# Elementwise work of two fused layers redistributed over VectorE, GpSimd and ScalarE

## The chip, the cores and the metric

One NeuronCore of a Trainium2 chip runs the whole program. The metric is the device time of one execution, in microseconds (us). Its engines are TensorE (matrix products; PE in the profile, PEld for its weight loads), VectorE (DVE), ScalarE (ACT), GpSimd (POOL) and SyncE (SP, which here issues nearly all DMAs). Each engine runs its own instructions strictly in the order of the program and waits on semaphores for the others.

## What is computed

The reference is a causal, windowed attention (4 batches, 8 heads, 576 tokens, head size 64) with a bias by distance, whose output is seen as `x` of 2304 tokens by 512, followed by two layers of the same form:

```
h = x @ w_in            # 512 -> 2048
g = where(h > 0, h, exp(min(h, 0)) - 1)      # layer 0 (ELU)
g = h * (1 / (1 + exp(-h)))                  # layer 1 (SiLU)
x = g @ w_out           # 2048 -> 512
```

The weights come as 64-bit floats. Everything is computed close to fp32 precision.

## The kernel before

**Products in halves.** TensorE multiplies a type that holds fewer bits than fp32. So every operand is split into an upper half (a ScalarE copy into that type) and a lower half (value minus upper half), and each product is three matmuls: upper by upper, upper by lower, lower by upper. For each operand tile there is thus one ScalarE instruction (`gh`, `w1h`, `wah`, ...) and one subtraction (`gl`, `w1l`, `wal`, ...).

**Stages.** The attention runs first and takes about 210 us; the first four feature tiles (`FIRST_F`, of 128 features each) of layer 0 are computed inside it, by `hidden` and `output`. What is left of that for the last token block ends at 240.4 us of the profiled execution. Then come 15 *steps* (the list `steps`, lines 657 and 658). A step is one block `b` of 768 tokens (`BIG`) with a *sweep* of six feature tiles, or four in the last sweep of layer 1. Layer 0 has two sweeps of three steps (steps 0 to 5), layer 1 three sweeps of three steps (steps 6 to 14). A step is a first part with quads and a second part with outputs.

**Quads.** `quad` (line 762) computes two feature tiles of `h` for 768 tokens with seven products in place of eight, as Strassen's scheme in Winograd's form does. The operands are sums of quarters of the weights (`s1` to `s4`, lines 188 to 191, in `part`) and sums of quarters of `x` (`t2`, `t3`, and two in place, lines 689 to 694, in `make`). A step of six features has three quads and 21 products of six matmuls. Each product's result is copied or added up by ScalarE (line 786) or VectorE (line 789).

**Activation.** Each quad gives four half-tiles of 128 features by 384 tokens, a full step twelve. `activate` (line 746) puts for each a chain of four entries in a list, and `chain` (line 740) emits one entry of every open chain after each product: `bent` (exp or sigmoid, line 752), the entry that calls `act` (lines 257 and 258 in layer 0, two VectorE instructions; line 260 in layer 1, one), `upper` (line 755) and `lower` (line 759). `lower` is GpSimd's, except for one half in layer 1.

**Outputs.** `outputs` (line 835 and on) multiplies the six `g` tiles with `w_out` (line 866), in eight groups (layer 0) or six (layer 1) of three pieces each, and adds each group into `acc` (line 879). The order is: `pieces` of the last step that were kept back (`pend`) are mixed among the first products, the last two products of a step among its first pieces.

**Weights.** A list of 64 `tasks` (one per 128-feature tile of `w_in` or `w_out`) goes strictly in order through `load_w` (a 512 KB DMA on SP, four raw buffers, `NRAW`), `rescale` (one GpSimd instruction, line 146, one ScalarE instruction, line 148), `sign` and `join` (VectorE, lines 153 and 158) and `part`. For `w_out` `part` is one upper and one lower half (`w1h`, `w1l`, line 168). For `w_in` two tasks make a *pair*: `wah`, `wal`, then the four sums, then `wb`, `wc`, `wd` with their halves. There is room for three pairs (`PAIRS`) and seven `w_out` tiles (`OUTS`). The room of a pair is given free when the last step of a sweep has used it, that of all `w_out` tiles of a sweep when the last group of that step is begun. So most of the next sweep's weights are made around the boundary between two sweeps: steps 2 and 3, 5 and 6, 8 and 9, 11 and 12. `weight_step` (line 215) is called by `between` after each product or output piece (`calls` counts them) and takes a few stages one task further, seven calls (`LAG`) after the load at the earliest; where a step needs a weight that is not there yet, a loop calls it until it is.

**Sums of x.** `make` (line 673) makes the seven operands of a step from `x`, in two halves `c` of the contraction. `begin` loads a half from DRAM in layer 0 (one buffer, so half 1 is loaded when half 0 is used up) and takes `acc` in layer 1. Its list of entries is emitted three at a time (`POPS`) by `between("y")`. In layer 0 the list begins with 21 empty entries (`POPS * LAG`), and 21 more stand between the two halves. After both, seven `keep` DMAs of 768 KB store the operands for a later step, in layer 0 and where a later step uses them. `make` runs for steps 0, 1, 2 (layer 0) and 6, 7, 8 (layer 1); the other steps reload the kept operands or use those of the step before. Step 0's list is put into the queue before the attention's leftover work is done; those of the others at the start of the outputs of the step before.

Of the kernel before, what the change touches and what calls it, by code (L numbers as in the profile page):

```python
# [13 lines left out]
AF = mybir.ActivationFunctionType  # L14
ALU = mybir.AluOpType
PSUM = bass.MemoryType.PSUM

P = 128
# [4 lines left out]
def f32(ap):  # L23
    return ap.bitcast(F32)
# [18 lines left out]
def attention_elu_silu_kernel(  # L43
# [14 lines left out]
    nc = tc.nc  # L58
# [5 lines left out]
    NKC = DM // P  # L64
# [12 lines left out]
    NRAW = 4  # L77
# [94 lines left out]
    def part(kind, layer, f):  # L172

        if kind == 1 or (layer == 0 and f < FIRST_F):
            top = raws.pop((kind, layer, f))[:, :, 1]
            pool = w_p if layer == 0 and f < FIRST_F else out_p[0]
            weights[kind, layer, f] = halves(pool, f"w{kind}", [(top, NKC * P)], nc.gpsimd)
            return
        if f % 2 == 0:
            t = raws[kind, layer, f]  # L180
            weights[kind, layer, f] = halves(pair_p[0], "wa", [(t[:, :, 1], NKC * P)], nc.gpsimd)
            return

        t0, t1 = raws.pop((kind, layer, f - 1)), raws.pop((kind, layer, f))
        w = NKC * P // 2
        a11, a12, a21, a22 = (f32(t[:, i * w:(i + 1) * w, 1]) for t in (t0, t1) for i in range(2))
        s1, s2, s3, s4 = (f32(t[:, i * w:(i + 1) * w, 0]) for t in (t0, t1) for i in range(2))
        nc.gpsimd.tensor_tensor(s1, a21, a22, op=ALU.add)
        nc.gpsimd.tensor_tensor(s3, a11, a21, op=ALU.subtract)
        nc.gpsimd.tensor_tensor(s2, s1, a11, op=ALU.subtract)  # L190
        nc.gpsimd.tensor_tensor(s4, a12, s2, op=ALU.subtract)
        weights[kind, layer, f] = (
            halves(pair_p[0], "wb", [(t1[:, w:2 * w, 1], w)], nc.vector),
            halves(pair_p[0], "wc", [(t0[:, :, 0], 2 * w)], nc.vector),
            halves(pair_p[0], "wd", [(t1[:, :, 0], 2 * w)], nc.vector))
# [19 lines left out]
    def weight_step(loaded=0, which=(4, 2, 3, 1), lag=1, last=64, apart=(1, 0, 1)):  # L215


        for i in which:
            if (stage[i] < min(last, stage[i - 1]) and (i < len(stages) or fits(stage[i]))
                    and calls[0] >= at[i - 1][stage[i]] + (lag, *apart)[i - 1]):  # L220
                if i == len(stages):
                    made[tasks[stage[i]][0]] += 1
                stages[i - 1](*tasks[stage[i]])
                at[i][stage[i]] = calls[0]
                stage[i] += 1
        while stage[0] < (loaded or min(stage[-1] + NRAW, len(tasks))):
            load_w(*tasks[stage[0]])
            at[0][stage[0]] = calls[0]
            stage[0] += 1
# [417 lines left out]
    def layers(fill):  # L647
# [25 lines left out]
        def make(k):  # L673

            layer, sw, b = steps[k]
            src = {}

            def begin(c):
                if layer == 0:
                    src[c] = t = t_p.tile([P, 2, BIG], F32, tag="xs", name="xs")  # L680
                    nc.sync.dma_start(t, x_dram[b][:, c::2, :])
                else:
                    src[c] = acc[b].rearrange("p (c t) -> p c t", c=NKC)[:, c::2, :]

            def sums(c):
                b11, b12, b21, b22 = (src[c][:, i, j * HALF:(j + 1) * HALF] for i in range(2) for j in range(2))
                t2, t3 = (t_p.tile([P, HALF], F32, tag=t, name=t) for t in ("t2", "t3"))
                src[c] = b11, b21, b22, b21, b12, t2, t3
                nc.gpsimd.tensor_tensor(t3, b22, b12, op=ALU.subtract)
                nc.gpsimd.tensor_tensor(b12, b12, b11, op=ALU.subtract)  # L690
                nc.gpsimd.tensor_tensor(t2, b22, b12, op=ALU.subtract)

            def last_sum(c):
                nc.gpsimd.tensor_tensor(src[c][1], src[c][1], src[c][5], op=ALU.subtract)

            def upper(c, i):
                if c == 0:
                    operand(k, i)
                nc.scalar.activation(combos[k, i][:, 0, c, :], src[c][i], AF.Copy)  # L699

            def lower(c, i):
                t = combos[k, i]
                nc.vector.tensor_tensor(t[:, 1, c, :], src[c][i], f32(t[:, 0, c, :]), op=ALU.subtract)

            def keep(i):
                d = scratch[layer, b, i] = dram_p.tile([P, 4 * HALF], F32, tag=f"d{layer}{b}{i}", name=f"d{layer}{b}{i}")
                nc.sync.dma_start(d, f32(combos[k, i].rearrange("p x c t -> p (x c t)")))

            def spread(c):
                out = [lambda: sums(c)]  # L710
                order = 1, 0, 5, 4, 6, 3, 2
                for x, i in enumerate(order):
                    out.append(lambda i=i: upper(c, i))
                    if x:
                        out.append(lambda i=order[x - 1]: lower(c, i))
                    if x == 2:
                        out.append(lambda: last_sum(c))
                out.append(lambda: lower(c, order[-1]))
# [6 lines left out]
            return begin_first, wait + out  # L725

        def reload(k, i):
            layer, sw, b = steps[k]
# [17 lines left out]
        def activate(layer, src, gh, gl, half, key):  # L746
            tiles = {}
            s = slice(half * HALF, (half + 1) * HALF)

            def bent():  # L750
                tiles["e"] = e = e_p.tile([P, HALF], F32, tag="e", name="e")
                nc.scalar.activation(e, src, AF.Exp if layer == 0 else AF.Sigmoid)  # L752

            def upper():
                nc.scalar.activation(gh[:, s], tiles["e"], AF.Copy)  # L755

            def lower():
                eng = nc.vector if layer == 1 and half == 0 else nc.gpsimd
                eng.tensor_tensor(gl[:, s], tiles["e"], f32(gh[:, s]), op=ALU.subtract)  # L759
            chains.append([bent, lambda: act(layer, src, tiles["e"]), upper, lower])  # L760

        def quad(k, q, last):

# [132 lines left out]

        begin, xs0 = make(0)
        begin()
        xtasks.extend(xs0)
        seq = list(fill)  # L900
        fill.clear()
        for pieces, after, _, _ in seq:
# [101 lines left out]
```

## Time and profile before

| | |
|---|---|
| median of 3 runs | 1026.32 us (1025.3 to 1027.28) |
| the profiled execution, device time | 1027.41 us |
| its span, first to last instruction | 1025.6 us |
| mean granted TensorE clock | 0.937 |
| busy: PE, DVE, ACT, POOL | 900.2, 633.1, 490.6, 427.2 us |
| chain that ended last, shares | PE 51%, DVE 15%, POOL 13%, ACT 9%, issue 7%, DMA 4% |

The busy times are of the whole span. TensorE is the busiest, but its busy time is not all work at full speed: the granted clock (PEclk) tells in tenths or hundredths what share of 2.4 GHz it ran at, and a matmul at 1.2 GHz is counted as busy for twice the time. The chain that ended last names what the end waited for, step by step; a share of VectorE, GpSimd and ScalarE in it means that TensorE stood still for them there.

### The profile page before, as it was taken

Reading aid. Unit: us, or ns where it says so; the run is one execution under the profiler, and the core shown is the slowest. Engines: PE = TensorE matmul, PEld = TensorE weight load, DVE = VectorE, ACT = ScalarE, POOL = GpSimd, SP = SyncE. Lnnn points to the kernel's source line nnn. Section 1 sums busy time; section 2 is a strip of 40 time slices with the busy share of each in tenths; the row PEclk is TensorE's granted clock in tenths of the full one; section 3 lists DMA queues with packets and bytes.
Section 4 is the critical chain, followed back from the end, with each engine's and each line's share of the span. In section 5 each row is a group of like instructions: output and inputs, shape, how many; then the busy total and the mean of one; then the engine's idle time right before and its main releaser. Section 6 shows DMA issues by size and latency. Waiting matters only on the chain.

```text
span 1025.6 us, 15310 instructions
## 1 busy us (share of the span) xinstructions
PE 900.2 (88%) x5520; PEld 798.6 (78%) x5520; DVE 633.1 (62%) x1241; ACT 490.6 (48%) x1155; POOL 427.2 (42%) x514
## 2 busy tenths in 40 slices
PE   6789999874649998897999839899989899999998
PEld 3667767653549998796999839698979698889997
DVE  6876567537666766777354678847377543474443
ACT  6676667534442536353233445555456332444322
POOL 7743333226554345755031763615264301252111
PEclk9889999996789998998999869999989899999999
DMA  9324353031731611236050128051324505024541
GB/s 303 104 73 150 115 156 124 12 113 64 299 118 43 235 31 42 72 116 234 1 216 1 46 93 305 20 215 66 150 82 157 222 3 214 5 78 184 186 184 62
DMA packets 54924, 125.52 MB, mean 122 GB/s; under 512 B 3648, under 2 KB 35648, under 8 KB 54848
## 3 DMA queue, kind: packets, MB, share of 16 engines
q1 hardware_dynamic: 54704, 124.40, 34.0%
q8 instruction: 44, 0.72, 0.3%
q14 instruction: 32, 0.26, 0.1%
q10 hardware_dynamic: 144, 0.13, 0.0%
HBM read 87.56 MB, written 36.96 MB: 121 GB/s over the span
## 4 chain that ended last, share of the span: by engine, by line
PE 51%; DVE 15%; POOL 13%; ACT 9%; issue 7%; DMA 4%; POOLq 0%; DVEq 0%; SPq 0%; ACTq 0%
PE y L866 24%; PE b L779 9%; PE c L779 5%; DVE e L257 3%; PE a L527 3%; DVE e L258 3%; PE h L274 3%; PE y L310 2%; POOL gl L759 2%; PE a L779 2%; DVE wraw L153 2%; DMA wraw<-in_moe_w_out_dram 2%; PE s L449 2%; PE pt L488 2%; ACT e L752 2%
## 5 line engine op out<-in xcount | busy, mean ns | idle before, releaser
L759 POOL TENSOR_TENSOR gl<-e,gh 128x384 fp32r<-128x384 f32 x120 | 131.1, 1095 | 321.6 <-ACT gh L755 297.0
L755 ACT ACTIVATE gh<-e 128x384 fp32r<-128x384 f32 x168 | 86.7, 523 | 103.8 <-DVE e L258 62.7
L866 PE MATMUL y<-w1h,gl 128*128 128x512 f32 (+1 forms) x292 | 115.2, 394 | 2.9 <-DVE gl L759 2.9
L866 PE MATMUL y<-w1h,gh 128*128 128x512 f32 (+1 forms) x292 | 114.8, 393 | 1.4 <-ACT gh L755 1.4
L866 PE MATMUL y<-w1l,gh 128*128 128x512 f32 (+1 forms) x292 | 114.5, 392 | 0.0
L866 PE MATMUL y<-gl,w1h 128*128 128x384 f32 x288 | 100.9, 350 | 15.2 <-POOL gl L759 15.2
L866 PE MATMUL y<-gh,w1h 128*128 128x384 f32 x288 | 100.3, 348 | 9.8 <-ACT gh L755 9.8
L508 POOL TENSOR_SCALAR p<-p,sm 128x192 f32<-128x192 f32 (+1 forms) x144 | 61.5, 445 | 100.7 <-DVE sm L466 90.8
L879 DVE TENSOR_TENSOR acc<-y,acc 128x384 f32<-128x384 f32 (+2 forms) x85 | 50.3, 605 | 81.1 <-PE y L866 81.1
L866 PE MATMUL y<-gh,w1l 128*128 128x384 f32 x288 | 99.8, 347 | 0.0
L257 DVE TENSOR_SCALAR e<-e 128x384 f32<-128x384 f32 (+2 forms) x92 | 51.9, 565 | 52.7 <-ACT e L752 30.9
L462 ACT ACTIVATE p<-p,neg 128x192 f32<-128x192 f32 (+1 forms) x144 | 62.9, 440 | 31.6 <-DVE neg L457 31.6
L153 DVE SCALAR_TENSOR_TENSOR wraw<-wraw 128x512 uint32<-128x512 uint32 x60 | 57.9, 965 | 26.2 <-POOL wraw L146 24.9
L866 PEld LDWEIGHTS y<-gl,w1h 128*128 128x128 f32 x288 | 56.5, 196 | 17.6 <-POOL gl L759 17.5
L786 ACT ACTIVATE hs<-b 128x384 f32<-128x384 f32 x42 | 20.2, 480 | 102.4 <-PE b L779 102.4
L866 PEld LDWEIGHTS y<-w1h,gl 128*128 128x128 f32 x292 | 56.0, 192 | 15.2 <-DVE gl L759 3.8
L752 ACT ACTIVATE e<-hs 128x384 f32<-128x384 f32 x84 | 44.1, 525 | 47.3 <-DVE hs L789 47.0
L866 PEld LDWEIGHTS y<-gh,w1h 128*128 128x128 f32 x288 | 57.0, 198 | 11.1 <-ACT gh L755 11.1
L866 PEld LDWEIGHTS y<-w1h,gh 128*128 128x128 f32 x292 | 56.0, 192 | 11.8 <-ACT gh L755 2.2
L168 POOL TENSOR_TENSOR w1l<-wraw,w1h 128x512 fp32r<-128x512 f32 x28 | 40.1, 1431 | 59.5 <-ACT w1h L167 42.9
L866 PEld LDWEIGHTS y<-w1l,gh 128*128 128x128 f32 x292 | 55.9, 191 | 9.6
L779 PE MATMUL b<-b,wah 128*128 128x384 f32 x168 | 44.0, 340 | 22.1 <-ACT b L699 20.1
(146 smaller groups left out, 2378.4 us busy)
## 6 DMA issues: line engine op xcount, KB each, us to landing
t<-d SPq DMA_DIRECT2D x24, 768.0 KB, 7.3
wraw<-in_moe_w_in_dram SPq DMA_DIRECT2D x32, 512.0 KB, 4.5
d<-t SPq DMA_DIRECT2D x20, 768.0 KB, 8.5
wraw<-in_moe_w_out_dram SPq DMA_DIRECT2D x28, 512.0 KB, 4.1
b<-d SPq DMA_DIRECT2D x18, 768.0 KB, 5.9
d<-b SPq DMA_DIRECT2D x15, 768.0 KB, 4.8
k<-in_k_dram SPq DMA_DIRECT2D x16, 384.0 KB, 5.2
v<-in_v_dram SPq DMA_DIRECT2D x18, 256.0 KB, 2.8
```

Of the source, the lines that this page charges most:

```text
L153: nc.vector.scalar_tensor_tensor(low, top, 0x80000000, low, op0=ALU.bitwise_and, op1=ALU.bitwise_or)
L168: eng.tensor_tensor(lo[:, o:o + w], f32(src), f32(h[:, o:o + w]), op=ALU.subtract)
L257: nc.vector.tensor_scalar(e, e, 1.0, -1.0, op0=ALU.min, op1=ALU.add)
L258: nc.vector.tensor_tensor(e, src, e, op=ALU.max)
L462: nc.scalar.activation(dst, dst, AF.Exp, bias=m, scale=-1.0, accum_out=a)
L508: nc.gpsimd.tensor_scalar(dst, dst, by, 1.0, op0=ALU.mult, op1=ALU.mult)
L752: nc.scalar.activation(e, src, AF.Exp if layer == 0 else AF.Sigmoid)
L755: nc.scalar.activation(gh[:, s], tiles["e"], AF.Copy)
L759: eng.tensor_tensor(gl[:, s], tiles["e"], f32(gh[:, s]), op=ALU.subtract)
L779: nc.tensor.matmul(t[name][:, 0:HALF], a[:, cs], x[:, j, c, :], start=(start and c == 0 and n == 0), stop=(c == 1 and n == 2), skip_group_ ...
L866: nc.tensor.matmul(t["ps"][:, 0:w], l, r, start=(f == 0 and x == 0), stop=(f == n - 1 and x == 2))
L879: nc.vector.tensor_tensor(dst, t["ps"][:, 0:w], dst, op=ALU.add)
```

## The change

All lower halves and sums of the layers that GpSimd made (`w1l`, `wal`, `s1` to `s4`, `gl`, the four sums of `x` per half) become VectorE instructions. GpSimd keeps the scaling of raw weights (line 146), the lower halves of the weights of the first four tiles, and what it did in the attention. In layer 0, two of the four half-tiles of a quad (`below`) get `min(h, 0)` from ScalarE, as minus `relu(-h)`, ahead of the exp, and then one VectorE instruction in place of two. In `weight_step` a raw buffer is loaded again only two calls after its last user was emitted. The list of sums of `x` loses its 21 leading empty entries; step 0's gets six.

```
--- before.py
+++ after.py
@@ -174,21 +174,22 @@
         if kind == 1 or (layer == 0 and f < FIRST_F):
             top = raws.pop((kind, layer, f))[:, :, 1]
             pool = w_p if layer == 0 and f < FIRST_F else out_p[0]
-            weights[kind, layer, f] = halves(pool, f"w{kind}", [(top, NKC * P)], nc.gpsimd)
+            eng = nc.gpsimd if pool is w_p else nc.vector
+            weights[kind, layer, f] = halves(pool, f"w{kind}", [(top, NKC * P)], eng)
             return
         if f % 2 == 0:
             t = raws[kind, layer, f]
-            weights[kind, layer, f] = halves(pair_p[0], "wa", [(t[:, :, 1], NKC * P)], nc.gpsimd)
+            weights[kind, layer, f] = halves(pair_p[0], "wa", [(t[:, :, 1], NKC * P)], nc.vector)
             return
 
         t0, t1 = raws.pop((kind, layer, f - 1)), raws.pop((kind, layer, f))
         w = NKC * P // 2
         a11, a12, a21, a22 = (f32(t[:, i * w:(i + 1) * w, 1]) for t in (t0, t1) for i in range(2))
         s1, s2, s3, s4 = (f32(t[:, i * w:(i + 1) * w, 0]) for t in (t0, t1) for i in range(2))
-        nc.gpsimd.tensor_tensor(s1, a21, a22, op=ALU.add)
-        nc.gpsimd.tensor_tensor(s3, a11, a21, op=ALU.subtract)
-        nc.gpsimd.tensor_tensor(s2, s1, a11, op=ALU.subtract)
-        nc.gpsimd.tensor_tensor(s4, a12, s2, op=ALU.subtract)
+        nc.vector.tensor_tensor(s1, a21, a22, op=ALU.add)
+        nc.vector.tensor_tensor(s3, a11, a21, op=ALU.subtract)
+        nc.vector.tensor_tensor(s2, s1, a11, op=ALU.subtract)
+        nc.vector.tensor_tensor(s4, a12, s2, op=ALU.subtract)
         weights[kind, layer, f] = (
             halves(pair_p[0], "wb", [(t1[:, w:2 * w, 1], w)], nc.vector),
             halves(pair_p[0], "wc", [(t0[:, :, 0], 2 * w)], nc.vector),
@@ -224,6 +225,8 @@
                 at[i][stage[i]] = calls[0]
                 stage[i] += 1
         while stage[0] < (loaded or min(stage[-1] + NRAW, len(tasks))):
+            if not loaded and stage[0] >= NRAW and calls[0] < at[-1].get(stage[0] - NRAW, 0) + 2:
+                break
             load_w(*tasks[stage[0]])
             at[0][stage[0]] = calls[0]
             stage[0] += 1
@@ -686,12 +689,12 @@
                 b11, b12, b21, b22 = (src[c][:, i, j * HALF:(j + 1) * HALF] for i in range(2) for j in range(2))
                 t2, t3 = (t_p.tile([P, HALF], F32, tag=t, name=t) for t in ("t2", "t3"))
                 src[c] = b11, b21, b22, b21, b12, t2, t3
-                nc.gpsimd.tensor_tensor(t3, b22, b12, op=ALU.subtract)
-                nc.gpsimd.tensor_tensor(b12, b12, b11, op=ALU.subtract)
-                nc.gpsimd.tensor_tensor(t2, b22, b12, op=ALU.subtract)
+                nc.vector.tensor_tensor(t3, b22, b12, op=ALU.subtract)
+                nc.vector.tensor_tensor(b12, b12, b11, op=ALU.subtract)
+                nc.vector.tensor_tensor(t2, b22, b12, op=ALU.subtract)
 
             def last_sum(c):
-                nc.gpsimd.tensor_tensor(src[c][1], src[c][1], src[c][5], op=ALU.subtract)
+                nc.vector.tensor_tensor(src[c][1], src[c][1], src[c][5], op=ALU.subtract)
 
             def upper(c, i):
                 if c == 0:
@@ -722,7 +725,7 @@
             out = spread(0) + [lambda: begin(1)] + wait + spread(1)
             if again(k):
                 out += [lambda i=i: keep(i) for i in range(7)]
-            return begin_first, wait + out
+            return begin_first, out
 
         def reload(k, i):
             layer, sw, b = steps[k]
@@ -747,17 +750,29 @@
             tiles = {}
             s = slice(half * HALF, (half + 1) * HALF)
 
+            below = layer == 0 and key[1] % 2 != half
+
             def bent():
                 tiles["e"] = e = e_p.tile([P, HALF], F32, tag="e", name="e")
-                nc.scalar.activation(e, src, AF.Exp if layer == 0 else AF.Sigmoid)
+                if below:
+                    nc.scalar.activation(e, src, AF.Relu, scale=-1.0)
+                    nc.scalar.activation(e, e, AF.Exp, scale=-1.0)
+                else:
+                    nc.scalar.activation(e, src, AF.Exp if layer == 0 else AF.Sigmoid)
+
+            def gated():
+                e = tiles["e"]
+                if below:
+                    nc.vector.scalar_tensor_tensor(e, e, -1.0, src, op0=ALU.add, op1=ALU.max)
+                else:
+                    act(layer, src, e)
 
             def upper():
                 nc.scalar.activation(gh[:, s], tiles["e"], AF.Copy)
 
             def lower():
-                eng = nc.vector if layer == 1 and half == 0 else nc.gpsimd
-                eng.tensor_tensor(gl[:, s], tiles["e"], f32(gh[:, s]), op=ALU.subtract)
-            chains.append([bent, lambda: act(layer, src, tiles["e"]), upper, lower])
+                nc.vector.tensor_tensor(gl[:, s], tiles["e"], f32(gh[:, s]), op=ALU.subtract)
+            chains.append([bent, gated, upper, lower])
 
         def quad(k, q, last):
 
@@ -896,7 +911,7 @@
 
         begin, xs0 = make(0)
         begin()
-        xtasks.extend(xs0)
+        xtasks.extend([None] * (2 * POPS) + xs0)
         seq = list(fill)
         fill.clear()
         for pieces, after, _, _ in seq:
```

## Rows read from the trace of the kernel before

**Rows 1.** section 1 of the page: busy time and span share by engine

```profile
...
PE 900.2 (88%) x5520; PEld 798.6 (78%) x5520; DVE 633.1 (62%) x1241; ACT 490.6 (48%) x1155; POOL 427.2 (42%) x514
...
```

**Rows 2.** stretches: us, busy (instructions) by engine, PEclk, DMA share, GB/s

```profile
...
210.00:240.40 30.40, 24.66 (x96) 19.31 (x95) 14.39 (x17) 10.86 (x21) 14.94 (x16) 0.89 0.28 95
210.00:331.70 121.70, 79.12 (x354) 69.55 (x353) 78.82 (x105) 49.67 (x100) 63.21 (x62) 0.82 0.36 128
...
379.90:500.00 120.10, 104.64 (x542) 100.51 (x542) 81.82 (x122) 50.91 (x101) 61.94 (x60) 0.91 0.28 99
500.00:547.70 47.70, 47.21 (x271) 46.89 (x271) 23.27 (x41) 15.93 (x33) 12.11 (x12) 1.00 0.31 116
547.70:675.20 127.50, 102.30 (x505) 95.06 (x505) 94.37 (x130) 63.98 (x130) 71.35 (x67) 0.88 0.31 112
675.20:721.60 46.40, 46.40 (x236) 42.14 (x235) 27.35 (x41) 25.24 (x53) 16.21 (x14) 1.00 0.33 136
721.60:828.40 106.80, 99.96 (x470) 88.59 (x469) 62.56 (x92) 50.99 (x103) 45.71 (x45) 0.94 0.36 133
...
874.80:925.20 50.40, 48.21 (x235) 43.64 (x234) 32.41 (x47) 22.49 (x46) 21.15 (x21) 0.97 0.12 42
240.40:1025.60 785.20, 692.98 (x3505) 643.22 (x3503) 480.95 (x723) 339.62 (x695) 319.59 (x305) 0.93 0.33 122
...
```

**Rows 3.** line 759: instructions, duration in ns min/median/max, first and last start

```profile
...
L759 POOL TENSOR_TENSOR gl<-e,gh x120: 993/1015/1562, 274.1 to 1011.2; 128x384 fp32r<-128x384 f32 x120
L759 DVE TENSOR_TENSOR gl<-e,gh x48: 542/550/1675, 627.0 to 1009.2; 128x384 fp32r<-128x384 f32 x48
...
```

**Rows 4.** line 168, same columns: lower halves of weights, on both engines

```profile
...
L168 POOL TENSOR_TENSOR w1l<-wraw,w1h x28: 1292/1328/1766, 268.2 to 937.3; 128x512 fp32r<-128x512 f32 x28
L168 POOL TENSOR_TENSOR wal<-wraw,wah x14: 1291/1317/1659, 213.7 to 901.7; 128x512 fp32r<-128x512 f32 x14
L168 DVE TENSOR_TENSOR wbl<-wraw,wbh x14: 440/1058/1300, 221.0 to 907.5; 128x256 fp32r<-128x256 f32 x14
...
L168 DVE TENSOR_TENSOR wdl<-wraw,wdh x14: 677/691/1502, 225.7 to 909.8; 128x512 fp32r<-128x512 f32 x14
...
```

**Rows 5.** groups by line and shape on GpSimd: busy, mean ns, idle before

```profile
...
L188 POOL TENSOR_TENSOR wraw<-wraw 128x256 f32<-128x256 f32 x14 | 15.0, 1073 | 1.5 <-DVE wraw L158 1.5
...
```

**Rows 6.** order of time, 396 to 408: start, us, instruction [idle before <-releaser]

```profile
...
397.76 1.21 POOL L759 TENSOR_TENSOR gl<-e,gh 128x384 fp32r<-128x384 f32 x1
...
398.13 1.26 DVE L258 TENSOR_TENSOR e<-hs,e 128x384 f32<-128x384 f32 x1
...
401.70 0.66 ACT L167 ACTIVATE wch<-wraw 128x512 fp32r<-128x512 f32 x1 [3.29 <-POOL wraw L190]
...
403.10 0.69 DVE L168 TENSOR_TENSOR wdl<-wraw,wdh 128x512 fp32r<-128x512 f32 x1
...
405.30 0.56 DVE L258 TENSOR_TENSOR e<-hs,e 128x384 f32<-128x384 f32 x1
...
405.68 1.01 PE L779 MATMUL b<-t,wdh 128*128 128x384 f32 x2 [3.66 <-ACT h L786]
405.77 0.35 DVE L257 TENSOR_SCALAR e<-e 128x384 f32<-128x384 f32 x1
...
```

**Rows 7.** waits over the whole run: in total, times, longest

```profile
...
POOL gl L759 <- ACT gh L755: 297.0, 74, 24.7
...
ACT wch L167 <- POOL wraw L190: 52.7, 14, 7.2
...
```

**Rows 8.** line 146 alone: stretch, GpSimd busy time (instructions), PEclk, DMA share

```profile
...
240.40:1025.60 785.20, 42.39 (x52) 0.93 0.33 122
...
```

**Rows 9.** line 258: instructions, duration in ns min/median/max

```profile
...
L258 DVE TENSOR_TENSOR e<-b,e x18: 556/558/558, 280.3 to 593.4; 128x384 f32<-128x384 f32 x18
...
```

**Rows 10.** line 752 on ScalarE, same columns

```profile
...
L752 ACT ACTIVATE e<-b x42: 463/475/492, 278.4 to 1006.4; 128x384 f32<-128x384 f32 x42
...
L752 ACT ACT_TABLE_LOAD  x1: 1283/1283/1283, 622.8 to 622.8; - x1
...
```

More of the change, by code (lines that the diff above doesn't have):

```diff
@@ L176, in part @@
             pool = w_p if layer == 0 and f < FIRST_F else out_p[0]
-            weights[kind, layer, f] = halves(pool, f"w{kind}", [(top, NKC * P)], nc.gpsimd)
+            eng = nc.gpsimd if pool is w_p else nc.vector
+            weights[kind, layer, f] = halves(pool, f"w{kind}", [(top, NKC * P)], eng)
             return
@@ L180, in part @@
             t = raws[kind, layer, f]
-            weights[kind, layer, f] = halves(pair_p[0], "wa", [(t[:, :, 1], NKC * P)], nc.gpsimd)
+            weights[kind, layer, f] = halves(pair_p[0], "wa", [(t[:, :, 1], NKC * P)], nc.vector)
             return
@@ L187, in part @@
         s1, s2, s3, s4 = (f32(t[:, i * w:(i + 1) * w, 0]) for t in (t0, t1) for i in range(2))
[L188 to L191, printed above, removed]
+        nc.vector.tensor_tensor(s1, a21, a22, op=ALU.add)
+        nc.vector.tensor_tensor(s3, a11, a21, op=ALU.subtract)
+        nc.vector.tensor_tensor(s2, s1, a11, op=ALU.subtract)
+        nc.vector.tensor_tensor(s4, a12, s2, op=ALU.subtract)
         weights[kind, layer, f] = (
@@ L226, in weight_step @@
         while stage[0] < (loaded or min(stage[-1] + NRAW, len(tasks))):
+            if not loaded and stage[0] >= NRAW and calls[0] < at[-1].get(stage[0] - NRAW, 0) + 2:
+                break
             load_w(*tasks[stage[0]])
@@ L688, in sums @@
                 src[c] = b11, b21, b22, b21, b12, t2, t3
-                nc.gpsimd.tensor_tensor(t3, b22, b12, op=ALU.subtract)
-                nc.gpsimd.tensor_tensor(b12, b12, b11, op=ALU.subtract)
-                nc.gpsimd.tensor_tensor(t2, b22, b12, op=ALU.subtract)
+                nc.vector.tensor_tensor(t3, b22, b12, op=ALU.subtract)
+                nc.vector.tensor_tensor(b12, b12, b11, op=ALU.subtract)
+                nc.vector.tensor_tensor(t2, b22, b12, op=ALU.subtract)
             def last_sum(c):
-                nc.gpsimd.tensor_tensor(src[c][1], src[c][1], src[c][5], op=ALU.subtract)
+                nc.vector.tensor_tensor(src[c][1], src[c][1], src[c][5], op=ALU.subtract)
             def upper(c, i):
@@ L724, in make @@
                 out += [lambda i=i: keep(i) for i in range(7)]
-            return begin_first, wait + out
+            return begin_first, out
         def reload(k, i):
@@ L748, in activate, with gated @@
             s = slice(half * HALF, (half + 1) * HALF)
+            below = layer == 0 and key[1] % 2 != half
             def bent():
                 tiles["e"] = e = e_p.tile([P, HALF], F32, tag="e", name="e")
-                nc.scalar.activation(e, src, AF.Exp if layer == 0 else AF.Sigmoid)
+                if below:
+                    nc.scalar.activation(e, src, AF.Relu, scale=-1.0)
+                    nc.scalar.activation(e, e, AF.Exp, scale=-1.0)
+                else:
+                    nc.scalar.activation(e, src, AF.Exp if layer == 0 else AF.Sigmoid)
+            def gated():
+                e = tiles["e"]
+                if below:
+                    nc.vector.scalar_tensor_tensor(e, e, -1.0, src, op0=ALU.add, op1=ALU.max)
+                else:
+                    act(layer, src, e)
             def upper():
@@ L757, in lower @@
             def lower():
-                eng = nc.vector if layer == 1 and half == 0 else nc.gpsimd
-                eng.tensor_tensor(gl[:, s], tiles["e"], f32(gh[:, s]), op=ALU.subtract)
-            chains.append([bent, lambda: act(layer, src, tiles["e"]), upper, lower])
+                nc.vector.tensor_tensor(gl[:, s], tiles["e"], f32(gh[:, s]), op=ALU.subtract)
+            chains.append([bent, gated, upper, lower])
         def quad(k, q, last):
@@ L898, in layers @@
         begin()
-        xtasks.extend(xs0)
+        xtasks.extend([None] * (2 * POPS) + xs0)
         seq = list(fill)
```

## The prediction

> **What bounds it now.** I read section 1 of the page first: TensorE is busy for 88% of the span, so some 125 us are idle, and part of the busy time is slow [rows 1]. Then the busy times by stretch, cut where a long run of outputs ends and the next step's first product begins in the order of time [rows 2]. Two kinds of stretch stand out. Step 4 (500.0 to 547.7) and step 7 (675.2 to 721.6) are clean: TensorE is busy throughout at a granted clock of 1.00, and a step takes 47.7 us in layer 0 and 46.4 us in layer 1. The other stretches hold the start or a boundary between two sweeps, at a clock of 0.82 to 0.97, and are longer than their steps need:
>
> - A, 210 to 331.7, what is left of the fused part and step 0: 121.7 us. It needs 24.7 us of matmuls up to 240.4 (TensorE's busy time there) and 47.7 for step 0, so 49.3 are excess.
> - B, 379.9 to 500, steps 2 and 3: 120.1 − 2 × 47.7 = 24.7.
> - C, 547.7 to 675.2, steps 5 and 6: 127.5 − 47.7 − 46.4 = 33.4.
> - D, 721.6 to 828.4, steps 8 and 9: 106.8 − 2 × 46.4 = 14.0.
> - E, 874.8 to 925.2, step 11: 4.0.
>
> That is 125.4 us, all that there is to win. What makes these stretches long is seen in durations. The same subtraction `gl` takes GpSimd 1015 ns in the median and VectorE 550, but VectorE's longest is 1675 [rows 3]; `wbl`, a quarter of a tile, takes VectorE 440 ns at best and 1058 in the median [rows 4]. The order of time shows why: at 397.76 GpSimd begins a `gl` of 1.21 us, and VectorE's line 258, begun 0.37 us later, takes 1.26 us; the same line takes 0.56 us at 405.30, when GpSimd is idle [rows 6]. With its second operand in PSUM it never takes over 558 ns [rows 9]. So a GpSimd instruction and a VectorE instruction on SBUF alone run one after the other here, and the boundary stretches are close to the sum of both engines' work: in B 81.8 + 61.9 us busy, waiting for each other included, in 120.1.
>
> The last link is ScalarE. For a pair it waits for GpSimd's sums, 52.7 us in 14 waits [rows 7], and its copies out of PSUM stand behind that: at 401.70 it has idled 3.29 us for `wch`, and at 405.68 TensorE has idled 3.66 us for ScalarE's `h` [rows 6].
>
> **The change, part by part.** *GpSimd to VectorE.* The prices on VectorE, undisturbed: 0.55 us for 128x384 [rows 3], 0.69 for 128x512 and 0.44 for 128x256 [rows 4]. Moved are 120 `gl` (66 us), 42 `w1l` and `wal` (29), 14 × 4 sums of weights (24.6) and 48 sums of `x` (26.4): 146 us more on VectorE. GpSimd loses these at 1.0, 1.3 and, for the dearest sum of weights, 1.07 us each [rows 3 to 5], and keeps in the layers 52 scalings, 42.4 us, 0.8 each [rows 8]. I still charge these to VectorE, as time in which it may stand.
>
> *The clamp.* In 36 half-tiles VectorE has one instruction in place of two. What goes is line 257, 0.35 us alone [rows 6]: 12.8 us in all. The new instruction has no row; it lies between that 0.35 and the 1.26 of a disturbed line 258, and I take line 258's 0.56, the same shape with the same two inputs [rows 6, 9]. ScalarE gets 36 more passes, at 0.46 to 0.53 us for an exp of that shape [rows 10], 3 us a step, up to 3.1 if a clamp costs as an exp does. ScalarE is busy for 49.7 of A's 121.7 us and for half of C [rows 2], so I cost it at nothing; its price without that cover is a rival. The Trainium skill speaks against this piece: ScalarE: Activation LUTs, under "Rules for kernel authors", says that max, min and relu belong on VectorE and not on ScalarE. The rows agree on the price of one (0.35 against about 0.5 us); by that rule the piece would give nothing, and the four steps of layer 0 in A, B and C would each lose its 2.1 us of VectorE, 8 us on the sum. Whether relu needs its own table no row shows. An exchange would cost 1.28 us [rows 10]; exps and copies alternate in this run without one.
>
> *Sums of x.* Step 0's list moves ahead by 15 entries, five calls; for steps 1 and 2 by 21, seven calls. With the four sums go seven ScalarE uppers, seven VectorE lowers, the 768 KB load of half 1 and later seven stores of 768 KB, all on SP's queue. They pass there the loads of raw weights, and on VectorE the halves of the first pairs. Nothing on POOL's queue is passed, as these sums leave it.
>
> *Loads two calls later.* A call is worth 47.7 us / 45 (21 products and 24 pieces) = 1.06 us. SP no longer stands at a load whose buffer is still being read, so that a load of `x` or a store behind it goes out: a gain of nothing to a few us in A. Against that the cycle of a raw buffer gets two calls longer. I take nothing for both and leave the loss to a rival.
>
> *A new wait.* VectorE now waits for ScalarE's `gh` itself, and `hs`, the gate of the next half-tile and weights queue behind it; TensorE waits for these. The bounds are 0 and what GpSimd waited, 297 us in 74 waits [rows 7], though mostly idle with nothing to do. I take 0, since VectorE already made 48 `gl` one call after their `gh`, half of them within 550 ns, which leaves them undisturbed [rows 3].
>
> **The sum.** VectorE's need, by counts. A step of layer 0: 12 `gl` 6.6, six half-tiles at 0.35 + 0.56 and six at 0.56, 8.8, nine adds 5.0, eight evictions 4.5: 24.9 us. A step of layer 1: 12 × 1.1 + 5.0 + 6 × 0.69 = 22.3. A pair: sign and join of both raws 2.76, sums 1.76, lower halves 2.51: 7.0. A `w_out` tile: 2.07. Six features: 33.4, with scalings 9.8. A `make`: 22 × 0.55 = 12.1.
>
> A: fused tail 6.9, halves and sums of three pairs 12.8, sign and join of 12 raws 16.6, six `w_out` halves 4.1, two `make`s 24.2, step 0 24.9, scalings 9.8: 99.3 of 121.7 us, saved 22.4.
>
> For B to E there are two ends. If work spreads evenly, the longer of TensorE and VectorE counts: B 93.0 against 95.4, so all 24.7 are saved; C 24.9 + 22.3 + 43.2 + 24.2 = 114.6 of 127.5, saved 12.9; D 87.8 against 92.8, saved 14.0; E 4.0. With A 78.0. If nothing spreads, only the outputs of the old sweep's last step and the quads of the new one's first count, one step of TensorE together. B: 24.8 (evictions 4.5, a fifth of the half-tiles 3.1, two pairs 14.0, scalings 3.2) and 31.7 (adds 5.0, 12.3, five `w_out` 10.4, 4.0), 8.8 over 47.7. C: with a `make` 36.9 and 30.0, 19.8 over 47.1. D: 23.9 and 30.0, 7.5 over 46.4. With 2 us each for the last wait the savings are 13.9, 11.6, 4.5 and 2.5 for E: 54.9 with A. No row prefers one of them: room opens from the second quad on, which spreads, but `w_out` has its room only at the end. I take the middle, 66.5 us. The profiled execution took 1027.4 us; 1027.4 − 66.5 = 960.9, and as it stands 1.1 above the median, **960 us**, with 942 to 978 as this case's own range (the ends are 948 and 971, and a few us for the loads and the clamp).
>
> **Rivals.** *TensorE alone is left* (0.10): VectorE's own instructions shorten and the clock stays at 1.00, so that 85% of the 125.4 go: 920 us. For it speaks that B and D need less of VectorE than of TensorE; against it A and C.
>
> *Loads held back* (0.12): 12 tasks go through four buffers, two more turns after the first, two calls each, 4 × 1.06 = 4.2 us at each of five places: 21 us, 981. For it: the boundaries are where weights are short. Against: in the clean steps TensorE waits for no weight (47.21 of 47.7 us busy [rows 2]), so raws lie ready when a boundary begins.
>
> *ScalarE in the way* (0.05): 3.1 us in each of six steps, 19 us, gives 979; with an exchange of tables before each clamp and each exp, 36 × 2 × 1.28 = 92 us of ScalarE, half on the path, 1006.
>
> *No relief* (0.05): the long VectorE durations come from something other than GpSimd and stay. Then its 94.4 us in C [rows 2] rise by what is moved there (18 `gl`, 16 sums of `x`, three pairs' sums and `wal`, six `w1l`: 30) to 124 of 127.5, and the same holds at the other places; only A and a part of B gain, some 25 us in all: 1001.
>
> *Slower* (0.06): VectorE and ScalarE wait for each other in the chains of half-tiles. If each moved `gl` holds VectorE for 1.1 us (its upper half and one more ScalarE pass ahead of that, 0.53 each [rows 10]), the twelve of steps 0, 2, 3, 5 and the six of steps 6, 8, 9, 11 cost 72 × 1.1 = 79 us: 1039. It decides from 0.92 us per `gl` on, where it eats the 66.5. For it: GpSimd's waits of 4 us each [rows 7]; against it the 550 ns median of VectorE's own `gl` [rows 3].
>
> **Numbers.** The forecast has 0.62. The range 926 to 1002 takes in the loads, the middle of ScalarE and no relief; left out are TensorE alone, slower, and ScalarE's dear end, some 0.18. About 0.2% can be told from no change here. Faster: 0.62 + 0.10 + 0.12 + 0.05 and most of no relief, 0.92; same 0.02; slower 0.06.
>
> **What would show it.** Right: VectorE's median for `wbl` near 440 ns and its longest `gl` far below 1675; no line of ScalarE waiting 3 us for sums; A near 99 us; C the longest of the boundaries; clock above 0.95. Wrong: idle time of VectorE before `gl` that ends at `gh`, over 0.5 us each; TensorE waiting for a raw weight's DMA; more than two table loads; clean steps longer than 47.7 and 46.4.

## The result and the profile after

973.1 us (median of 4 runs, 972.32 to 975.27) against 1026.8 for the kernel before in the same comparison: a ratio of 0.9478, with a 95% interval of 0.9452 to 0.9504. The forecast was 960 us in a range of 926 to 1002; 53.7 us were won where 66.5 had been forecast.

Busy time and share of the span (970.3 us) by engine, as in [rows 1]:

```profile
...
PE 879.8 (91%) x5520; PEld 782.0 (81%) x5520; DVE 655.6 (68%) x1471; ACT 506.6 (52%) x1191; POOL 136.9 (14%) x248
...
```

GpSimd has gone from 427 to 137 us. VectorE took over its work and is busy for only 22.5 us more: what it got is nearly balanced by the time by which its own instructions became shorter. The durations show that, line 774 (`gl`) and line 168 (the weights' lower halves), in ns min/median/max, as [rows 3, 4]:

```profile
...
L774 DVE TENSOR_TENSOR gl<-e,gh x168: 542/551/989, 263.8 to 959.3; 128x384 fp32r<-128x384 f32 x168
...
```

```profile
...
L168 DVE TENSOR_TENSOR w1l<-wraw,w1h x28: 678/693/1145, 258.7 to 883.8; 128x512 fp32r<-128x512 f32 x28
...
L168 DVE TENSOR_TENSOR wbl<-wraw,wbh x14: 418/418/421, 223.6 to 852.4; 128x256 fp32r<-128x256 f32 x14
...
```

`wbl` had a median of 1058 ns and a longest of 1300; now all 14 lie between 418 and 421. The longest `gl` on VectorE has fallen from 1675 to 989.

The stretches, with the columns of [rows 2] (us; PE, PEld, DVE, ACT, POOL busy with instructions; PEclk, DMA share, GB/s), cut at the same places of the program, A, B, step 4, C, step 7, D, E, and the layers as a whole:

```profile
...
210.00:314.80 104.80, 75.28 (x358) 67.00 (x357) 84.41 (x155) 54.56 (x111) 11.58 (x14) 0.90 0.47 167
361.70:467.10 105.40, 97.82 (x542) 94.84 (x541) 79.38 (x148) 53.72 (x108) 9.08 (x12) 0.98 0.32 113
467.10:514.10 47.00, 47.00 (x272) 47.00 (x272) 23.94 (x47) 18.65 (x39) 0.00 (x0) 1.00 0.31 118
514.10:632.00 117.90, 100.76 (x506) 93.24 (x505) 93.61 (x179) 66.13 (x136) 9.64 (x12) 0.93 0.33 122
632.00:678.40 46.40, 46.40 (x236) 42.15 (x236) 27.47 (x55) 25.46 (x53) 0.00 (x0) 1.00 0.39 160
678.40:776.60 98.20, 94.12 (x469) 84.03 (x469) 69.95 (x125) 51.10 (x103) 10.33 (x12) 1.00 0.37 133
823.00:871.20 48.20, 46.87 (x235) 41.88 (x235) 34.84 (x64) 22.53 (x46) 3.12 (x4) 1.00 0.13 45
238.30:970.30 732.00, 673.46 (x3505) 627.19 (x3503) 497.65 (x932) 353.08 (x725) 39.52 (x50) 0.97 0.36 131
...
```

A is 104.8 us for 121.7, B 105.4 for 120.1, C 117.9 for 127.5, D 98.2 for 106.8, E 48.2 for 50.4: 52.0 us together of the 55.3 by which the span is shorter. The clean steps 4 and 7 take 47.0 and 46.4 us, where they took 47.7 and 46.4. The granted clock in A to E is 0.90 to 1.00 where it was 0.82 to 0.97. Of the 55.3 us, 20.4 are time in which TensorE was busy, as the same 5520 matmuls took 900.2 us and take 879.8 at this higher clock; the other 34.9 are idle time of TensorE that is gone.

What TensorE and ScalarE wait for now (in total, times, longest):

```profile
...
ACT wch L167 <- DVE wraw L191: 20.5, 11, 5.6
...
PE y L881 <- DVE gl L774: 13.9, 6, 5.0
...
PE b L794 <- ACT b L702: 12.8, 1, 12.8
...
DVE gl L774 <- ACT gh L771: 10.3, 14, 1.6
...
```

ScalarE's wait for the sums is down from 52.7 us in 14 to 20.5 in 11. VectorE's new wait for `gh` is 10.3 us for 168 `gl`. TensorE's longest waits in the layers are one in A and two of the six for `gl`, both in C. They are not new. In the kernel before (the first line from the whole run, the second from 520 to 640 us alone) they were

```profile
...
PE b L779 <- ACT b L699: 20.1, 1, 20.1
...
PE y L866 <- POOL gl L759: 10.9, 2, 7.0
...
```

so that the wait in A has become shorter by 7.3 us; those in C, 9.8 us now, have hardly changed in length, but it is VectorE that ends them where it was GpSimd.

In A TensorE stands 12.8 us inside step 0's first product: the matmuls on half 0 of the operands ran at 238.3 us, and ScalarE's copy of half 1 is late. In order of time:

```profile
...
245.42 0.56 DVE L692 TENSOR_TENSOR t<-xs 128x384 f32<-128x384 f32 x1 [2.83 <-DMA xs<-xd]
...
248.64 0.68 ACT L167 ACTIVATE wch<-wraw 128x512 fp32r<-128x512 f32 x1 [5.59 <-DVE wraw L191]
...
250.81 0.92 ACT L702 ACTIVATE b<-xs 128x384 fp32r<-128x384 f32 x2
...
251.78 0.69 PE L794 MATMUL b<-b,wah 128*128 128x384 f32 x1 [12.77 <-ACT b L702]
...
```

The sums of `x` wait for their load at 245.42; the third pair's sums stand behind them on VectorE, ScalarE's `wch` has idled 5.59 us for these at 248.64, and the copies that step 0 needs come behind `wch`.

In C, in the outputs of step 5, TensorE idles 4.97 and 4.86 us for a `gl`:

```profile
...
557.75 0.69 DVE L168 TENSOR_TENSOR wal<-wraw,wah 128x512 fp32r<-128x512 f32 x1 [1.17 <-ACT wah L167]
558.36 0.55 DVE L774 TENSOR_TENSOR gl<-e,gh 128x384 fp32r<-128x384 f32 x1
...
558.97 0.69 PE L881 MATMUL y<-gl,w1h 128*128 128x384 f32 x1 [4.97 <-DVE gl L774]
...
559.77 0.55 DVE L692 TENSOR_TENSOR t<-acc 128x384 f32<-128x384 f32 x1
...
561.89 0.42 DVE L189 TENSOR_TENSOR wraw<-wraw 128x256 f32<-128x256 f32 x1
...
563.36 0.42 DVE L168 TENSOR_TENSOR wbl<-wraw,wbh 128x256 fp32r<-128x256 f32 x1
...
564.33 0.69 DVE L168 TENSOR_TENSOR wdl<-wraw,wdh 128x512 fp32r<-128x512 f32 x1
...
564.93 0.55 DVE L774 TENSOR_TENSOR gl<-e,gh 128x384 fp32r<-128x384 f32 x1
...
565.54 0.69 PE L881 MATMUL y<-gl,w1h 128*128 128x384 f32 x1 [4.86 <-DVE gl L774]
...
```

Between the two `gl` VectorE is never idle: lines 692 and on are the sums of `x` for step 6, lines 189 to 192 and 168 the third pair. `gl` is an instruction of 0.55 us that stands in a queue of over 6 us.

### The profile page after: what moved, and what is told of

Read it like the earlier page. It is cut to its first block, busy times and chain, and to the rows that moved or that the text cites. A ratio compares the mean times of both kernels' runs of the same rounds, so it can differ in the third digit from the quotient of the medians.

```text
span 970.3 us, 15097 instructions
## 1 busy us (share of the span) xinstructions
PE 879.8 (91%) x5520; PEld 782.0 (81%) x5520; DVE 655.6 (68%) x1471; ACT 506.6 (52%) x1191; POOL 136.9 (14%) x248
## 4 chain that ended last, share of the span: by engine, by line
PE 65%; DVE 16%; ACT 10%; issue 4%; DMA 4%; POOL 1%; SPq 0%; DVEq 0%; ACTq 0%; POOLq 0%
PE y L881 31%; PE b L794 12%; PE c L794 6%; PE a L530 4%; PE y L313 3%; PE a L794 3%; PE h L277 2%; DMA wraw<-in_moe_w_out_dram 2%; PE pt L491 2%; PE s L452 2%; DVE wraw L153 2%; ACT p L465 1%; DVE gl L774 1%; DVE e L261 1%; DVE w1l L168 1%
## 5 line engine op out<-in xcount | busy, mean ns | idle before, releaser
L146 POOL TENSOR_SCALAR wraw<-wraw 128x512 f32<-128x512 f32 x60 | 46.2, 771 | 596.7 <-DMA wraw<-in_moe_w_in_dram 314.6
L881 PE MATMUL y<-w1h,gl 128*128 128x512 f32 (+1 forms) x292 | 113.1, 387 | 0.7 <-DVE gl L774 0.7
L881 PE MATMUL y<-w1h,gh 128*128 128x512 f32 (+1 forms) x292 | 112.8, 386 | 0.0
L881 PE MATMUL y<-gl,w1h 128*128 128x384 f32 x288 | 99.3, 345 | 13.2 <-DVE gl L774 13.2
L774 DVE TENSOR_TENSOR gl<-e,gh 128x384 fp32r<-128x384 f32 x168 | 92.0, 557 | 12.9 <-ACT gh L771 10.3
L801 ACT ACTIVATE hs<-b 128x384 f32<-128x384 f32 x42 | 20.4, 486 | 110.9 <-PE b L794 110.9
L794 PE MATMUL b<-b,wah 128*128 128x384 f32 x168 | 43.6, 339 | 14.1 <-ACT b L702 12.8
L881 PEld LDWEIGHTS y<-gh,w1l 128*128 128x128 f32 x288 | 55.6, 193 | 0.0
L794 PE MATMUL b<-t,wbh 128*128 128x384 f32 x168 | 45.0, 349 | 10.2 <-DVE hs L804 10.2
```

Source lines behind the costliest of these rows:

```text
L146: nc.gpsimd.tensor_scalar(f32(top), f32(top), 2.0 ** -112, 1.0, op0=ALU.mult, op1=ALU.mult)
L774: nc.vector.tensor_tensor(gl[:, s], tiles["e"], f32(gh[:, s]), op=ALU.subtract)
L794: nc.tensor.matmul(t[name][:, 0:HALF], a[:, cs], x[:, j, c, :], start=(start and c == 0 and n == 0), stop=(c == 1 and n == 2), skip_group_ ...
L801: nc.scalar.activation(t[name], t[src][:, 0:HALF], AF.Copy)
L881: nc.tensor.matmul(t["ps"][:, 0:w], l, r, start=(f == 0 and x == 0), stop=(f == n - 1 and x == 2))
```

## The experiments

All times are medians; the ratio is to the kernel before, run on the same chip in the same comparison.

**1. Only the change of engines.**

```
...
-            if not loaded and stage[0] >= NRAW and calls[0] < at[-1].get(stage[0] - NRAW, 0) + 2:
-                break
...
-            return begin_first, out
+            return begin_first, wait + out
...
-            below = layer == 0 and key[1] % 2 != half
+            below = False
...
-        xtasks.extend([None] * (2 * POPS) + xs0)
+        xtasks.extend(xs0)
```

> Only the move of lower halves and sums from GpSimd to VectorE; clamp, load rule and early sums are undone. Theory (the 53.7 us gained come from VectorE no longer standing while GpSimd works): most of the gain stays, 978 to 992 us, the rest being the early sums at the start (up to 12 us in stretch A). Rival (the earlier sums, the load order and the clamp carry half or more): 1000 us or above.

982.44 us, ratio 0.9554 (0.9538 to 0.9569). 4.5 of the 5.2% come from the move of engines alone. The three other pieces together bring 0.8%. Undone one at a time (experiments 2 to 4) they sum up to about 0.2%, so either they help each other or this is noise: each of these ratios is known to some 0.2%.

**2. Without the clamp on ScalarE** (`below = False` alone).

> The change without ScalarE's clamp: the 36 half-tiles have VectorE's two instructions again. Theory of the sum (VectorE bound at the boundaries, 2.1 us a step in steps 0, 2, 3, 5): 976 to 982 us. Rival (ScalarE's extra passes stand in the way, the gain fell short of 66 us because of them): 965 to 970 us.

975.67 us, ratio 0.9483 (0.9459 to 0.9507): not to be told from the change (0.9478), and outside both ranges. The 8 us of the sum are not there, nor is a gain without the clamp; an effect of 3 us, the low end of the theory, is not excluded.

**3. Loads at once** (without the two lines with `break`).

> The change without the rule that holds a raw buffer's load back for two calls. If the rule lets SP's other DMAs pass, as the load of half 1 in stretch A: 975 to 985 us. If holding back delays weights at five boundaries (4.2 us each): 953 to 968 us. If neither: within 2 us of 973.

978.24 us, ratio 0.9516 (0.9494 to 0.9538); the intervals overlap a little. A gain by the rule of some five us is likely but not certain. In the profiled executions step 3 takes 55.9 us here and 53.7 in the change, step 9 51.5 and 49.5 (51.5 in experiment 1 too, the other run without the rule); C goes the other way, with 115.9 and 117.9. The 21 us of the rival that weights come late are out. Why those steps gain was not followed further.

**4. The lists of x late** (`wait + out` and `xtasks.extend(xs0)` as before).

> The change with the 21 empty entries ahead of the lists of layer 0 again. Theory (step 0 starts when half 1 of its operands is there, and that hangs on when the list begins): stretch A grows by 5 to 12 us, total 978 to 985. Rival (the load of half 1 and VectorE's queue set the start anyway): within 2 us of 973.

971.76 us, ratio 0.9453 (0.9431 to 0.9474): no loss, if anything a gain. A is 103.7 us for 104.8. The load of half 1, by the order of time on SP's queue, goes out at 242.91 here and at 238.03 in the change:

```profile
...
242.91 0.56 SPq L684 DMA_DIRECT2D xs<-xd  x1
...
```

```profile
...
238.03 0.56 SPq L684 DMA_DIRECT2D xs<-xd  x1
...
```

(first this experiment, then the change). So the list did move ahead as planned, and the load was 4.9 us earlier, but step 0 did not go on earlier: its first matmul on half 1 begins at 250.55 us here and at 251.78 in the change. What stood behind the sums of `x` had to be done in any case.

**5. GpSimd at work beside VectorE.** GpSimd gets two small subtractions per `gl`, on a tile of its own, whose making is left out here.

```
                 nc.vector.tensor_tensor(gl[:, s], tiles["e"], f32(gh[:, s]), op=ALU.subtract)
+                for _ in range(2):
+                    nc.gpsimd.tensor_tensor(idle[0], idle[0], idle[0], op=ALU.subtract)
```

> The change, and beside each of the 168 gl GpSimd does two small subtractions on a tile of its own that nothing reads and no one waits for. Theory (a GpSimd instruction with two inputs from SBUF and a VectorE instruction on SBUF alone run one after the other): VectorE's gl and gates that meet one take 0.3 to 0.6 us longer, their longest over 1.0 us, and the time rises by 10 to 35 us. Rival (GpSimd was only slow in the chain, and VectorE's long durations had another cause): VectorE's durations stay and the time is within 3 us of 973.

990.49 us, ratio 0.9635 (0.9592 to 0.9678): 17.4 us slower for work that nobody waits for. It is 178.7 us of GpSimd (group by line and shape: busy, mean ns, idle before):

```profile
...
L780 POOL TENSOR_TENSOR idle<-idle 128x128 f32<-128x128 f32 x336 | 178.7, 532 | 23.6
...
```

The `gl` on VectorE (min/median/max) and A and C by stretch:

```profile
...
L778 DVE TENSOR_TENSOR gl<-e,gh x168: 543/552/1045, 265.9 to 976.8; 128x384 fp32r<-128x384 f32 x168
...
```

```profile
...
210.00:323.80 113.80, 82.55 (x367) 72.86 (x366) 93.68 (x156) 56.81 (x116) 51.08 (x80) 0.87 0.44 158
525.70:647.30 121.60, 101.44 (x506) 93.10 (x505) 101.34 (x179) 66.04 (x136) 46.25 (x76) 0.93 0.30 109
...
```

In A VectorE is busy for 93.7 us with 156 instructions where the change has 84.4 with 155, and A is 9.0 us longer; in C 101.3 against 93.6 with the same 179, and C is 3.7 us longer. The median of `gl` stays, since most meet no GpSimd instruction; its mean goes from 557 to 594 ns. That its longest is over 1.0 us, as expected, says little, as it was 0.99 in the change. What happens when the two meet is seen in the order of time:

```profile
...
284.60 0.83 POOL L780 TENSOR_TENSOR idle<-idle 128x128 f32<-128x128 f32 x1
285.09 0.75 DVE L778 TENSOR_TENSOR gl<-e,gh 128x384 fp32r<-128x384 f32 x1
...
290.47 0.40 POOL L780 TENSOR_TENSOR idle<-idle 128x128 f32<-128x128 f32 x1
290.53 0.76 DVE L778 TENSOR_TENSOR gl<-e,gh 128x384 fp32r<-128x384 f32 x1
...
```

The first `gl` begins 0.49 us after GpSimd's subtraction, the second 0.06 us after it, and both end 0.41 to 0.42 us after the subtraction has ended. So it is with all 31 `gl` of this run that take over 600 ns: each begins while GpSimd is at work and ends 400 to 418 ns after GpSimd's instruction, whenever it began. In the kernel before, in the change and here no `gl` of VectorE that overlaps no GpSimd instruction takes over 560 ns.

VectorE's wait for the scalings, which now stand behind this work on GpSimd, explains nothing: 7.7 us before line 153 in all, 7.4 in the change. This is the mechanism by itself: a `gl` that VectorE begins while GpSimd is at work ends a fixed time after GpSimd's instruction, without any dependence between the two.

**6. `gl` back on GpSimd.**

```
-                nc.vector.tensor_tensor(gl[:, s], ...)
+                eng = nc.vector if layer == 1 and half == 0 else nc.gpsimd
+                eng.tensor_tensor(gl[:, s], ...)
```

> The change with gl on GpSimd again as before (120 of 168); weights and sums of x stay on VectorE. Theory: half of the moved GpSimd time returns (120 of some 240 us), with VectorE freed of 66 us that it then loses again by standing: 985 to 1000 us. Rival (VectorE is too full now and gl would be better off on GpSimd): 960 to 970 us.

984.45 us, ratio 0.958 (0.9532 to 0.9628): 11 us of the gain are lost, a little under what was expected. In step 6 alone it is 62.1 us against 52.2, and there the clock falls to 0.92:

```profile
...
580.20:642.30 62.10, 49.80 (x236) 44.73 (x236) 44.66 (x77) 31.77 (x64) 12.96 (x12) 0.92 0.40 147
...
```

At the beginning of step 6 both kernels are level (580.2 and 579.8 us): A and steps 2 and 3 lose 5 us together, and step 5 wins 4.8 (60.9 against 65.7). There TensorE waits 1.5 us for `gl` and 5.2 for `gh` in place of 9.8 for `gl`, which no longer stands in VectorE's queue. So the rival, that `gl` is better off on GpSimd, is right for step 5 and wrong on the whole.

**7. The weights back on GpSimd** (`w1l`, `wal`, `s1` to `s4`; `gl` and the sums of `x` stay on VectorE).

> The change with the weights' sums and lower halves (w1l, wal, s1 to s4) on GpSimd again; gl and the sums of x stay on VectorE. These are some 95 us of GpSimd's work, all of it at the start and the boundaries, against 120 us of gl of which a good part lies in steps that had nothing to lose. Theory (what counts is work on both engines where weights are made, and ScalarE waiting for the sums): 990 to 1005 us, more than putting gl back (984.45). Rival (the count of microseconds on GpSimd decides): 980 to 984 us.

989.29 us, ratio 0.9635 (0.961 to 0.966): 16 us, just under the range of the theory and well above the rival's. Between 240 and 1020 us GpSimd is busy for 137.3 us here, 174.2 with `gl` back and 39.5 in the change: 98 us of work on weights cost 16 us, 135 of `gl` 11. The two ratios' intervals overlap, so that it is only likely that the weights cost more in all; per microsecond on GpSimd they cost more also at the ends of these intervals. The waits name the chain of the kernel before again:

```profile
...
ACT wch L167 <- POOL wraw L191: 34.9, 14, 3.2
...
PE y L881 <- DVE gl L774: 18.1, 7, 6.7
...
```

ScalarE stands 34.9 us for GpSimd's sums in 14 waits.

**8. The lists of layer 1 four calls later.**

```
-            return begin_first, out
+            return begin_first, [None] * (4 * POPS if layer == 1 else 0) + out
```

> The change with 12 empty entries (four calls) ahead of the lists of layer 1. In step 5 TensorE stands 4.98 and 4.86 us for gl that queue on VectorE behind the sums of x for step 6. Theory (bunching in VectorE's queue is what the middle of my sum left out): those 9.8 us mostly go, 964 to 970 us. Rival (VectorE has too much to do there whatever the order; it then ends later at step 6's start): 971 to 976 us.

967.21 us, ratio 0.9414 (0.9372 to 0.9456). Steps 5 and 6:

```profile
...
516.00:575.80 59.80, 51.33 (x272) 49.14 (x271) 50.64 (x100) 35.15 (x73) 6.10 (x7) 0.94 0.25 88
575.80:626.80 51.00, 46.96 (x237) 41.89 (x236) 42.93 (x80) 30.95 (x63) 3.91 (x5) 1.00 0.47 174
...
```

Together 110.8 us against 117.9: 7.1 us of C were a matter of order. The total's interval touches that of the change; C is as short in experiments 9 (112.3) and 12 (110.7), and 115.9 to 120.4 in the profiled executions of experiments 1 to 4 and 11.

**9. Eight calls later** (`8 * POPS`).

> As the run with 12 empty entries ahead of layer 1's lists (967.21 us), with 24 of them (eight calls). If step 5's outputs still wait for gl because of the sums of x (4.38 us of its 5.3): 962 to 966 us. If the pairs' instructions are in front of it instead: 966 to 972 us, since step 6 then waits for its operands.

967.51 us, ratio 0.9434 (0.941 to 0.9457). Step 5 gains again, and step 6 gives it back:

```profile
...
514.10:570.60 56.50, 50.58 (x273) 48.41 (x272) 46.47 (x92) 32.76 (x69) 5.94 (x7) 0.97 0.19 66
570.60:626.40 55.80, 48.70 (x235) 43.31 (x234) 46.08 (x86) 32.62 (x67) 4.49 (x5) 0.97 0.42 155
...
```

**10. Chains first.** As experiment 8, and during output pieces no weight stage is emitted while a chain is open.

```
             calls[0] += 1
+            if where == "y" and chains:
+                return
             weight_step(0, ((4, 1), (2, 3))[calls[0] % 2], LAG)
```

> As the run with 12 empty entries (967.21 us), and during output pieces no weight stage is emitted while a half-tile's chain is open, so that gl stands ahead of the pairs on VectorE. If order alone makes those waits: stretch C loses up to 5 us and the total is 960 to 965 us. If VectorE's amount of work sets the boundary: 965 to 972 us, the wait then moves to the next step's first quads.

976.59 us, ratio 0.9526 (0.9495 to 0.9558), worse than both ranges. Step 5 is almost clean at 51.0 us, step 6 needs 68.4:

```profile
...
515.20:566.20 51.00, 48.08 (x272) 46.80 (x271) 40.68 (x80) 29.70 (x63) 4.04 (x4) 1.00 0.13 42
566.20:634.60 68.40, 52.02 (x238) 46.58 (x237) 53.88 (x101) 36.29 (x73) 6.00 (x8) 0.88 0.43 158
...
```

and TensorE now waits in step 6 for ScalarE's copies behind the late pairs:

```profile
...
PE b L794 <- ACT h L801: 7.7, 2, 7.5
PE b L794 <- ACT hs L801: 4.8, 1, 4.8
...
```

Both steps together take 119.4 us, against 110.8 in experiment 8 and 117.9 in the change. So order decides where TensorE waits, and it can make the two steps longer as well as shorter; work that is held back in step 5 is paid for in step 6.

**11. Scaling on VectorE too** (line 146 with `nc.vector`).

> The change with the scaling of raw weights on VectorE too, so that GpSimd does nothing in the layers. If standing for GpSimd's 50 scalings (0.8 us each) costs VectorE more than doing them itself (one input, 0.4 to 0.5 us each): 966 to 972 us. If VectorE's fuller queue at the boundaries weighs more: 974 to 985 us.

973.74 us, ratio 0.9459 (0.9406 to 0.9511): the same as the change, and between the two ranges. A scaling takes VectorE 426 ns, about half of GpSimd's 771:

```profile
...
L146 DVE TENSOR_SCALAR wraw<-wraw 128x512 f32<-128x512 f32 x60 | 25.5, 426 | 4.7 <-DMA wraw<-in_moe_w_out_dram 4.7
...
```

A falls to 102.6 us, but step 6 rises from 52.2 to 56.4. It fits that VectorE spends on the scalings what it gains by never standing for GpSimd; this was not tried by itself.

**12. Both lists later**: experiments 4 and 8 together.

> The run with 12 empty entries ahead of layer 1's lists (967.21 us), and the 21 empty entries ahead of layer 0's lists again. If the place of layer 0's list is worth nothing, because VectorE is full between 214 and 252 us either way: 964 to 969 us, ratio 0.940 to 0.945, the first product of step 0 within 3 us of 254. If the early list is worth something after all: 970 to 975 us.

963.14 us, ratio 0.9381 (0.9361 to 0.94). That is faster than the change (0.9452 to 0.9504) and the lowest time of all, though its interval touches that of experiment 8. A is 104.9 us, C 110.7; step 0's first matmul on half 1 begins at 251.2 us, 251.8 in the change. The time is just below the range that was expected if the place of layer 0's list is worth nothing, and far from the other: putting that list ahead gained nothing and may have cost a few us.

## Why the prediction was right, and where it was off

*What bounded it* held. The gain sits in the five stretches named, and the clean steps hardly changed. That VectorE and GpSimd run one after the other on SBUF, read from durations alone, is shown by experiment 5: more work on GpSimd without any dependence makes VectorE's own longer and the kernel slower. "No relief" is out. In the chain that ended last GpSimd's share has gone from 13% to 1%, while VectorE's stayed (15 and 16%).

What no run parts is the gain of the move (46 us in experiment 1) into its two causes: VectorE's own instructions are held up less, and chains for which TensorE and ScalarE wait no longer go through an engine that takes 1015 ns where VectorE takes 551. Experiment 5 has the first alone, at a tenth of a microsecond for each on GpSimd; at that price the 290 us less on GpSimd would be 28 of the 46 us, an estimate, as the price depends on where the work lies (experiments 6 and 7).

*The prices on VectorE* held to a few ns: 551 for `gl`, 693 for `w1l` and 418 for `wbl`, where 0.55, 0.69 and 0.44 us had been taken. The counts held to 5%: in B VectorE is busy for 79.4 us, the sum of 93.0 without its 9.8 of scalings being 83.2. Moving the scalings to VectorE is worth nothing net (experiment 11).

*The sum was 12.8 us too high.* The terms for A, B and C fall short by 5.5, 4.6 and 2.7 us, those for D and E by 1.8 together; that the forecast is not further off is owed to 3.3 us that came in stretches to which the sum gave nothing. (These are read from the profiled spans, 55.3 us apart; the medians are 53.7 us apart.)

- A: the sum took VectorE's 99.3 us as if it were busy from 210 on. It was busy for 84.4 of 104.8. It stood for a load, and ScalarE and TensorE for what was queued behind that load. Of the 22.4 us forecast 16.9 came.
- B and C: the middle between "spreads" and "does not spread" was taken, 19.3 and 12.3 us; 14.7 and 9.6 came, B near the low end (13.9) and C below its own (11.6). D (8.6 for a middle of 9.3) and E (2.2 for 3.3) lie near the middle. In C the instructions did not spread because the sums of `x`, the third pair and `gl` are emitted at the same output pieces, and `gl`, for which TensorE waits, has no precedence. Experiments 8 to 10 show how much of that is order: 7 us can be had, and another order loses them again. What holds B back was not tried.

*Two of the signs named ahead failed.* A was to come near 99 us and is 104.8. No line of ScalarE was to wait 3 us for sums, and `wch` still waits 20.5 us in all, up to 5.6 at a time, now for VectorE. The chain that the prediction called the last link has thus become shorter and is not gone. The other signs of being right came, and none of those of being wrong.

*The clamp.* The sum took 8 us of relief in A, B and C, which lie within the terms above. Experiment 2 does not find them (975.67 against 973.1, within the intervals). Why VectorE could not use the 0.35 us of each was not tried. The Trainium skill (ScalarE: Activation LUTs, "Rules for kernel authors") has such a clamp on VectorE and not on ScalarE. By that rule, the prediction said, the piece gives nothing, and experiment 2 agrees with it, as far as 2.6 us within the noise can.

*Loads two calls later* had been taken as nothing. The rival that saw 21 us lost is out; some 5 us may have been won (experiment 3).

*Sums of x* were worth nothing or less (experiment 4). The prediction had named what they pass on VectorE's queue, the halves of the first pairs, and did not draw the conclusion: what is moved ahead of the pairs can make the pairs late. With the list late `wch` waits 2.6 us in A for its sums, with the list early 9.7.

*The new wait* was rightly taken as nothing: 10.3 us for 168 `gl`, 0.06 us each, where 0.92 would have been needed for "slower". The reason given for it was weak: a median of 550 ns tells how long a `gl` ran and not how long VectorE stood before it. TensorE's wait for `gl` behind other work on VectorE is what the prediction missed: it said that work would queue there and gave it no price, though TensorE already waited 10.9 us in C for GpSimd's `gl`.

*ScalarE in the way* is out: two table loads as before, and no gain without the clamp. (Its 0.53 us for an exp is not in [rows 10], where `e<-b` takes 463 to 492 ns; the same line on `hs` takes 527 in the median.)

## What to carry to other kernels

Where an instruction of one engine has two well separated durations, look at what the engine beside it does in the long ones before moving work to it to balance the load: here 290 us less on GpSimd cost VectorE 22.5 us. What such work costs depends on where it lies: the weights' 98 us on GpSimd, all at the start and the boundaries, cost 16 when put back, 135 us of `gl` 11. After such a move look at what stands in the queue that has become full: here four calls' delay of work for a later step won 7 us at one boundary, and holding back more of it lost them again in the next step.

## What was not expected of the hardware

Scaling 512 columns from SBUF takes VectorE 426 ns and GpSimd 771 on average in the change, yet the kernel takes as long with the one as with the other (experiment 11). And GpSimd's small subtraction of 128 columns takes 532 ns, so that 336 of them, 178.7 us of an engine that has little else to do there, lengthened the kernel by 17.4 us: about a tenth of their time.
